# A planned transformer block: loads in a fixed order on two queues, pads on ScalarE, first projections by piece

## The chip, the cores and the metric

The kernel runs on one core of a Trainium2 chip. A core has TensorE (matrix products into PSUM, called PE in the profile), VectorE (DVE), ScalarE (ACT), GpSimd (POOL) and SyncE (SP), which run side by side and wait for each other through semaphores, and 16 DMA engines, which are given work through the queues of SP and ACT. The metric is the time of one launch in microseconds (us), the median of several runs.

## The reference

The block works on x of 2048 rows by 448 columns in bfloat16, with 16 heads of 28. Cut to what is computed:

```python
mod = (silu(c) @ w_mod).reshape(1, 6, 1, -1)          # c: 1 x 448, w_mod: 448 x 2688
sa, ca, ga, sb, cb, gb = (mod[:, i] for i in range(6))
h = layernorm(x) * (1 + ca) + sa
x = x + ga * A(h)          # attention, output projection wo
h = layernorm(x) * (1 + cb) + sb
x = x + gb * B(h)          # (sigmoid(h @ w_gate) * (h @ w_up)) @ w_down, 1792 wide

# A, for each of 4 segments s of 512 rows, per head (phi(t) = t + 1 for t > 0, else exp(t)):
a_dot = softmax(qs @ ks.T * scale + causal_mask) @ vs
a_mem = (phi(qs) @ M) / (phi(qs) @ z + 1e-6)
o = sigmoid(beta) * a_mem + (1 - sigmoid(beta)) * a_dot
M = M + phi(ks).T @ vs;  z = z + phi(ks).sum(rows)
```

## The kernel before

The kernel is a list of nodes for a planner (class `Graph`, L61 to L202). Each node is one piece of work for one engine (or for the better of two), with a duration in ns, the nodes it depends on, the buffers it takes (`Slot`) and a priority. `Graph.run` plays the engines forward with these durations and writes the instructions out in the order in which its nodes started. Every engine then runs its own instructions strictly in that order. So the order on each engine, the queue of SP included, is set when the kernel is built, from the table `PRM` (a priority for each kind of work and segment) and from estimates such as a load's bytes by a rate. `lock` keeps a VectorE node and a GpSimd node from being planned at the same time.

The work of a segment is:

- `ln1`: statistics (L543, L544), inverse root on GpSimd (L550, L551), normalized rows `xn` (L556). Segment 0 is turned by TensorE (L612) and scaled and shifted out of PSUM (L622, L624). Segments 1 to 3 are turned by DMA transposes on SP (L566), scaled and shifted in place (`modulated`, L576, L578), and copied by two more DMAs so that each half of the partitions holds other columns ("shifts", L583, L586).
- `proj`: Q and K (L654), 64 rows of the array for each half, and V (L667).
- `attention`: for four chunks of four heads, logits (L732), exponentials on ScalarE (L746, L752), causal masks on GpSimd (L759) or VectorE (L762); then `unit`: the product with V (L787, "PV"), the memory part (L798) and eight VectorE steps up to the transposed output `oT` (L836). There are 16 units.
- `memory`: phi of the keys, a DMA transpose on SP (`pk`, L690), a product (L696), and copies or sums into `M_sb`; TensorE and VectorE have these in their order too.
- `wo_ln2`: output projection (L850), residual (L853), second norm, turned by DMA like `ln1`.
- `ffn`: gate and up (L869), tanh (L874), product (L876), down projection (L888), residual (L894), store.

Loads are issued where the planner puts them: a load waits until the planned backlog of the DMA is under 1.5 us, so that loads and transposes alternate on SP. Weights of Q, K and V are loaded into halves of 64 partitions, gate into the lower half and up into the upper. Weights of the output and down projections are scaled by ga and gb once (L528, GpSimd or VectorE). GpSimd also fills pads (L402 to L406), and makes masks. wq and wk are spread into `wqk` by copies (L494, L496). Fourteen matmuls on zeros come first (L901).

Of the kernel before, what the change touches and what calls it, by code (L numbers as in the profile page):

```python
# [13 lines left out]
P = 128  # L14
ENGINES = ("PE", "ACT", "DVE", "POOL", "SP")
SWITCH = 100
LAND = 1400
BACKLOG = 1500

PRM = {  # L20
    "lg": (342668, 163718, 862290, 444708),
    "ex": (11292, 58782, -81945, -99549),
    "mask": (714759, 688992, 570356, 838873),
    "wo": (-115857, 165597, 132082, 82856),
    "ln2": (34672, 175804, -62256, 229718),
    "tanh": (49047, 57056, -189565, -190444),
    "f": (459427, 351186, 97650, 519018),
    "dn": (-246990, 125472, 5139, -149550),
    "phi": (347979, 71782, 70153, 194215),
    "t": (177082, 2744, 97268, 333494),  # L30
    "ln1": (103674, -21841, -146667, -66581),
    "mem": (-329139, -251836, -266191, -362099),
    "pj": (46451, -491526, -367702, 12439),
    "ot": (260037, 371245, 206466, 283138),
    "ev": (-163934, -86827, -16960, -49902),
    "gu": (231026, 437056, 117153, 563291),
}
STAY = 3248
# [22 lines left out]
class Graph:  # L61


    LAG = {"PE": {"PE": 0, "ACT": 205, "DVE": 205, "POOL": 205, "SP": 205},
           "ACT": {"PE": 200, "ACT": 0, "DVE": 170, "POOL": 190, "SP": 170},
           "DVE": {"PE": 180, "ACT": 150, "DVE": 0, "POOL": 170, "SP": 120},
           "POOL": {"PE": 150, "ACT": 110, "DVE": 90, "POOL": 0, "SP": 100}}
# [22 lines left out]
    def ready_at(self, n, e):  # L90
        t = n.release
        if n.move is not None and n.move > 300:
            t = max(t, self.ring - BACKLOG)
        for d in n.deps:
            t = max(t, d.end + d.lag + self.gap(d.eng, e))
        return t

# [30 lines left out]
    def run(self):  # L128
# [10 lines left out]
        self.ring = 0.0  # L139
        order, t, done = [], 0.0, 0  # L140
        while done < len(self.nodes):
            moved = False
            for e in ENGINES:
# [6 lines left out]
                narrow = None  # L150
                for n in ready:
                    got = self.place(n, t, narrow)
# [5 lines left out]
                    for s, i in zip(n.take, got):  # L158
                        s.at = i
                        for w in range(s.width):  # L160
                            self.free[s.pool][i + w] = float("inf")
# [10 lines left out]
                    if n.move is not None:  # L172
                        self.ring = max(self.ring, n.end) + n.move
                        n.lag = self.ring - n.end + LAND
# [4 lines left out]
                    for s in {id(x): x for x in (*n.take, *n.use)}.values():  # L179
                        if all(u.end is not None for u in s.users):  # L180
                            f = max(u.end + (u.lag if u.move is not None else 0) for u in s.users) + 120
                            for w in range(s.width):
                                self.free[s.pool][s.at + w] = f
# [9 lines left out]
            times = [x for x in (*at.values(), held) if x > t]  # L193
            times += [r for e in ENGINES for n in avail[e] if (r := self.ready_at(n, e)) > t]
            times += [f for fs in self.free.values() for f in fs if t < f < float("inf")]
# [10 lines left out]
def kernel(  # L206
# [36 lines left out]
    NWARM = 14  # L243
# [34 lines left out]
    c_col = const.tile([CP, NK], BF16, name="c_col")  # L278
# [4 lines left out]
    beta_t = const.tile([P, NHC, 4], BF16, name="beta_t")  # L283
# [4 lines left out]
    cols = const.tile([P, 4, 2, NK], F32, name="cols")  # L288
# [12 lines left out]
    xn_r = ring("xn", NXN, [P, HR + NK * P], BF16)  # L301
# [23 lines left out]
    silu_bc = U_r[0:CP, 0].rearrange("p i b e j -> p (i b e j)")[:, 0:NK * P].rearrange("p (k o) -> p k o", o=P)  # L325
    fT_flat = fT_r[:].rearrange("p n l -> p (n l)")
# [3 lines left out]
    def load(eng, dst, src, size, deps=(), prio=0, use=(), take=(), rate=230.0):  # L330
        def fn():
            (nc.sync if eng == "SP" else nc.scalar).dma_start(dst, src)
        return add(eng, 520, fn, deps, prio=prio, use=use, take=take, move=size / rate)

    def pr(kind, s):
        return PRM[kind][s]
# [13 lines left out]
    def load_x(eng, t0, t1, prio):  # L350
        n = load(eng, x_sb[:, t0:t1, :], x_dram[t0 * P:t1 * P, :].rearrange("(t p) d -> p t d", p=P),
                 (t1 - t0) * P * D * 2, prio=prio)
# [5 lines left out]
    def load_wm(eng, j0, nj, flat, prio, deps=()):  # L358
        t = flat[0:CP, 0:NK * nj * D].rearrange("p (k n) -> p k n", k=NK)
        n = load(eng, t, wm_cols[:, :, j0 * D:(j0 + nj) * D], CP * NK * nj * D * 2, prio=prio, deps=deps,  # L360
                 rate=230.0 if nj == 1 else 300.0)
# [4 lines left out]
    def load_half(eng, dst, half, w, prio, c0=0, c1=NC, rate=200.0):  # L366
        r = slice(half * HR, (half + 1) * HR)
        n = w.shape[1]
        return load(eng, dst[r, c0:c1, 0:n], w[c0 * HR:c1 * HR, :].rearrange("(c p) n -> p c n", p=HR),
                    HR * (c1 - c0) * n * 2, prio=prio, rate=rate)  # L370

    l_c = load("SP", c_col[:], c.rearrange("o (p k) -> p (o k)", p=CP), 20000, prio=2 * BIG)
    load_x("SP", 0, 1, 2 * BIG - 100)
    load_x("ACT", 1, 2, 2 * BIG - 100)
    load_x("SP", 2, 3, 2 * BIG - 200)
    load_x("ACT", 3, 4, 2 * BIG - 200)
    load_wm("SP", 0, 2, pT_r[:].rearrange("p n h w -> p (n h w)"), 2 * BIG - 300)
    W_qk = [load_half("ACT", wqk_st, 0, A_wq, 2 * BIG - 300), load_half("SP", wqk_st, 1, A_wk, 2 * BIG - 400)]
    W_v = [load_half("SP", wvv, i, A_wv, BIG - 60) for i in range(2)]
    lp = BIG - 100  # L380
    load_x("SP", TPS, 2 * TPS, lp)
    l_beta = load("SP", beta_t[:], A_beta.partition_broadcast(P), 8000, prio=lp - 1)
# [8 lines left out]
    def pads_fn():  # L391
        nc.vector.memset(xn_r[:, :, 0:HR], 0.0)
        nc.vector.memset(xn_r[:, :, HR + D:], 0.0)
        nc.vector.memset(wqk[:, :, :, Dh:HP], 0.0)

    wz = qT_r[:, 0, 0, :]
    n_wz = dve(200, lambda: nc.vector.memset(wz, 0.0), prio=BIG)
    n_ident = pool_op(700, ident_fn, prio=BIG)
    n_pads = dve(300, pads_fn, prio=BIG - 1, lock=True)

    def vpad_fn(i):
        nc.gpsimd.memset(vt_r[:, i, :, :, Dh:HP], 0.0)  # L402
        nc.gpsimd.memset(vt_r[:, i, :, :, Dh:Dh + 1], 1.0)
    n_vpad = [pool_op(700, lambda i=i: vpad_fn(i), prio=BIG - 5) for i in range(NV)]
    n_wopad = pool_op(1500, lambda: nc.gpsimd.memset(wo_sb[:], 0.0), prio=BIG - 4)
    n_opad = pool_op(400, lambda: nc.gpsimd.memset(O_r[:, :, :, Dh:HP, :], 0.0), prio=BIG - 6)  # L406
    l_wo = [load("SP", wo_sb[h * HP:h * HP + Dh, :, :],
                 A_wo.rearrange("(c h e) n -> h e c n", h=4, e=Dh)[h], Dh * NHC * D * 2, [n_wopad], prio=lp - 4)
            for h in range(4)]
# [11 lines left out]
    n_masks = pool_op(1900, masks_fn, prio=BIG - 7)  # L421
# [11 lines left out]
    n_hsel = pool_op(900, hsel_fn, prio=BIG - 9)  # L433


    def silu_fn():
        nc.vector.tensor_scalar(th[:], th[:], 0.5, 0.5, op0=ALU.mult, op1=ALU.add)
        nc.vector.tensor_tensor(silu[:], th[:], c_col[:], ALU.mult)
    n_th = act(200, lambda: nc.scalar.activation(th[:], c_col[:], AF.Tanh, scale=0.5), [l_c], prio=BIG)
    n_silu = dve(220, silu_fn, [n_th], prio=BIG, lock=True)  # L440
    n_sbc = dve(340, lambda: nc.vector.tensor_copy(
        silu_bc, silu[:].rearrange("p (k o) -> p k o", o=1).to_broadcast([CP, NK, P])), [n_silu], lock=True)

    def mod_cols(j, vi, both, prio):
        b = bank()

        def mm():
            for kc in range(NK):
                r = P if kc < NK - 1 else HR
                for k in range(NK):  # L450
                    nc.tensor.matmul(pf(b)[0:r, kc:kc + 1], lhsT=wm_at[j][:, k, kc * P:kc * P + r],
                                     rhs=silu[:, k:k + 1], start=(k == 0), stop=(k == NK - 1))
            for kc in range(NK if both else 0):
                for k in range(NK):
                    if kc:
                        nc.tensor.matmul(pf(b)[:, NK + kc:NK + kc + 1], lhsT=wm_at[j][:, k, kc * P - HR:kc * P + HR],
                                         rhs=silu[:, k:k + 1], start=(k == 0), stop=(k == NK - 1))
                    else:
                        nc.tensor.matmul(pf(b)[HR:P, NK:NK + 1], lhsT=wm_at[j][:, k, 0:HR], rhs=silu[:, k:k + 1],
                                         start=(k == 0), stop=(k == NK - 1), tile_position=(0, HR))  # L460
        n = add("PE", (32 if both else 16) * 40, mm, [n_silu, wml[j]], take=[b], prio=prio, mode="F")

        def ev():
            parts = [(0, NK - 1, P, 0), (NK - 1, NK, HR, 0)] + ([(NK, NK + 1, P, 1), (NK + 1, 2 * NK, P, 1)] if both else [])
# [479 lines left out]
```

## Time and profile before

| What | Value |
|---|---|
| Median of 3 runs | 270.43 us (269.98 to 270.99) |
| Profiled execution, its own time | 269.01 us |
| Its span, first to last instruction | 267.3 us |
| TensorE busy | 236.7 us (89%) |
| VectorE busy | 201.2 us (75%) |
| ScalarE busy | 153.6 us (57%) |
| GpSimd busy | 56.4 us (21%) |
| Read from HBM | 11.07 MB |

The page of a profile gives busy time of each engine, then the same in 40 slices, the DMA queues, the chain of work that ended last, and the costliest groups of instructions with the mean duration of one and the idle time before them. A busy TensorE may still run slowly, since the profile counts a matmul as busy from its start to its modelled end, and since its clock (PEclk) can be at half. Durations in the page come from this one execution.

### The profile page before, as it was taken

How to read it: one execution, taken by the hardware profiler on the slowest of the kernel's cores; microseconds unless marked ns; L12 is line 12 of the kernel's file. 1: busy time of each engine (PE TensorE's matmuls, PEld its weight loads, DVE VectorE, ACT ScalarE, POOL GpSimd, SP SyncE). 2: the span in 40 equal slices, each digit the busy share in tenths (PEclk: the TensorE clock that was granted, in tenths of full speed). 3: DMA queues.
4: the chain of work that ended last, by engine and by line, in shares of the span. 5: the costliest groups of instructions: out<-in, count | busy, mean ns of one | idle time of the engine just before them, and what ended most of it. 6: DMA issues, size and time to landing. Idle time of an engine off the chain costs nothing. (4 is left out here: it accounts for less than half of the span.)

```text
span 267.3 us, 5480 instructions
## 1 busy us (share of the span) xinstructions
PE 236.7 (89%) x2130; PEld 108.0 (40%) x2130; DVE 201.2 (75%) x478; ACT 153.6 (57%) x182; POOL 56.4 (21%) x110
## 2 busy tenths in 40 slices
PE   7289936999862899989999999999999999899995
PEld 2253512443330334435644443564444435354342
DVE  5658895998999798999699998769967674243331
ACT  1266964999986668974689834577534223033210
POOL 6701340111673570006020003400000211000000
PEclk9958965999995599999999999999999999999999
DMA  4999999999021333400432113130010212400011
GB/s 115 186 228 221 141 189 210 205 203 331 14 42 39 70 60 67 64 16 6 80 88 56 22 20 76 40 89 20 17 37 0 22 39 54 105 0 2 1 33 35
DMA packets 34737, 21.71 MB, mean 81 GB/s; under 512 B 23000, under 2 KB 32920, under 8 KB 34712
## 3 DMA queue, kind: packets, MB, share of 16 engines
q1 hardware_dynamic: 33960, 20.74, 38.5%
q10 hardware_dynamic: 752, 0.63, 0.9%
q8 instruction: 16, 0.26, 0.4%
q14 instruction: 9, 0.07, 0.1%
HBM read 11.07 MB, written 1.84 MB: 48 GB/s over the span
## 5 line engine op out<-in xcount | busy, mean ns | idle before, releaser
L869 PE MATMUL ps<-hT,wgu 64*128 64x512 bf16 x784 | 93.4, 383 | 1.1 <-DMA hT<-hT 0.8
L874 ACT ACTIVATE tt<-ps 128x512 f32<-128x512 f32 x56 | 33.3, 595 | 61.2 <-PE ps L869 60.5
L746 ACT ACTIVATE pT<-ps 128x2048 bf16<-128x2048 f32 x32 | 60.0, 1878 | 9.6 <-PE ps L732 8.7
L869 PEld LDWEIGHTS <-wgu 64*128 64x128 bf16 x784 | 40.4, 95 | 49.1 <-issue 12.8
L876 DVE SCALAR_TENSOR_TENSOR fT<-tt,ps 128x512 bf16<-128x512 f32 x56 | 38.1, 683 | 27.6 <-ACT tt L874 26.7
L888 PE MATMUL ps<-wd_sb,fT 128*128 128x448 bf16 x224 | 45.8, 353 | 0.2 <-ACT aT L804 0.2
L654 PE MATMUL ps<-hT,wqk 64*128 64x512 bf16 x224 | 31.0, 413 | 3.3 <-DMA hT<-hT 1.6
L759 POOL TENSOR_SCALAR_AFFINE_SELECT pT<-pT 128x512 bf16<-128x512 bf16 x25 | 15.9, 647 | 83.3 <-ACT pT L746 63.8
L888 PEld LDWEIGHTS <-fT 128*128 128x128 bf16 x224 | 20.7, 98 | 21.8 <-issue 4.4
L550 POOL TENSOR_SCALAR rs<-mv 128x1 f32<-128x1 f32 (+1 forms) x23 | 5.4, 237 | 78.8 <-DVE mv L544 78.7
L732 PE MATMUL ps<-qT,kT 28*128 28x512 bf16 (+3 forms) x256 | 17.0, 320 | 4.8 <-ACT pT L752 2.6
L543 DVE BATCH_NORM_STATS2 st<-x_sb 128x6 f32<-128x448 bf16 x32 | 19.5, 609 | 2.0 <-DMA x_sb<-in_A_x_dram 1.7
L654 PEld LDWEIGHTS <-wqk 64*128 64x128 bf16 x224 | 13.5, 100 | 18.3 <-issue 9.9
L894 DVE TENSOR_TENSOR ot<-ps,x_sb 128x448 bf16<-128x448 f32 x16 | 9.8, 615 | 10.9 <-PE ps L888 10.6
L762 DVE TENSOR_TENSOR pT<-pT,cmask 128x512 bf16<-128x512 bf16 x39 | 16.6, 450 | 1.2 <-ACT pT L746 0.9
L556 DVE TENSOR_SCALAR xn<-x_sb,mv,rs 128x448 bf16<-128x448 bf16 x32 | 14.7, 490 | 2.8 <-POOL rs L551 2.8
L850 PE MATMUL ps<-wo_sb,oT 128*128 128x448 bf16 x64 | 14.3, 354 | 1.4 <-DVE fT L876 0.8
L752 ACT ACTIVATE pT<-ps 128x2048 bf16<-128x2048 f32 x8 | 15.0, 1879 | 0.7 <-PE ps L732 0.6
L551 POOL TENSOR_TENSOR rs<-rs,mhalf 128x1 f32<-128x1 f32 (+1 forms) x23 | 14.9, 646 | 1.9
L787 PE MATMUL ps<-pT,vt 128*32 128x512 bf16 (+3 forms) x256 | 12.3, 315 | 3.0 <-DVE pT L762 3.0
L732 PEld LDWEIGHTS <-kT 28*128 28x128 bf16 x256 | 5.0, 94 | 22.4 <-issue 22.0
L667 PE MATMUL ps<-wvv,hT 64*128 64x448 bf16 x112 | 12.0, 350 | 0.2 <-ACT pT L746 0.2
(96 smaller groups left out, 249.3 us busy)
## 6 DMA issues: line engine op xcount, KB each, us to landing
hT<-hT SPq DMA_DIRECT2D x7, 256.0 KB, 3.4
out_dram<-ot SPq DMA_DIRECT2D x16, 112.0 KB, 1.7
x_sb<-in_A_x_dram SPq DMA_DIRECT2D x3, 448.0 KB, 11.4
wgu<-in_B_w_gate_dram SPq DMA_DIRECT2D x3, 448.0 KB, 5.2
wgu<-in_B_w_up_dram SPq DMA_DIRECT2D x3, 448.0 KB, 6.4
hT<-hT SPq DMA_DIRECT2D x7, 192.0 KB, 2.7
wd_sb<-in_B_w_down_dram SPq DMA_DIRECT2D x2, 448.0 KB
pT<-in_w_mod_dram SPq DMA_DIRECT2D x1, 784.0 KB
```

What stands on the lines that cost most here:

```text
L543: nc.vector.bn_stats(st_r[:, st.at, :], src)
L551: nc.gpsimd.tensor_tensor(r, r, mhalf[:, 0:w], ALU.pow)
L654: nc.tensor.matmul(pf(b), lhsT=w, rhs=chunk(hT, cc, half), start=(cc == 0), stop=(cc == NC - 1))
L732: nc.tensor.matmul(ps[:, lg.at + hs, o:o + nq], lhsT=kT_r[r, k.at, hcs[u], kb * P:(kb + 1) * P], rhs=qT_r[r, q.at, hcs[u], kb * P:L], star ...
L746: nc.scalar.activation(pT_r[:, pTs[units[0]].at, :, w0:w0 + L], ps_, AF.Exp, scale=scale)
L752: nc.scalar.activation(dst, ps_.rearrange("p h (u w) -> p u h w", u=2), AF.Exp, scale=scale)
L759: nc.gpsimd.affine_select(out=blk, in_=blk, compare_op=ALU.is_ge, fill=0.0, base=0, pattern=[[0, 4], [1, P]], channel_multiplier=-1)
L762: nc.vector.tensor_tensor(blk, blk, cmask[:].rearrange("p (o k) -> p o k", o=1).to_broadcast([P, 4, P]), ALU.mult)
L869: nc.tensor.matmul(pf(b), lhsT=wgu[half * HR:(half + 1) * HR, cc, fs], rhs=chunk(hT, cc, half), start=(cc == 0), stop=(cc == NC - 1))
L874: a = act(485, lambda gp=gp, tt=tt: nc.scalar.activation(tt_r[:, tt.at, :], pf(gp), AF.Tanh, scale=0.5), [n], use=[gp, tt], prio=pr("tanh" ...
L876: f = dve(597, lambda up=up, tt=tt, ft=ft: nc.vector.scalar_tensor_tensor(fT_r[:, ft.at, :], tt_r[:, tt.at, :], 1.0, pf(up), op0=ALU.add, ...
L888: nc.tensor.matmul(pf(b)[:, 0:D], lhsT=fT_r[:, fts[fc].at, t * P:(t + 1) * P], rhs=wd_sb[:, fc, :], start=(fc == 0), stop=(fc == NFC - 1))
```

## The change

All loads are written in one fixed order of priority (`first(i)`), on two queues, and a load's landing time is now a number written by hand (`land`) in place of bytes by a rate. The order is c, x of segment 0, the first two parts of w_mod (half on each queue), wq and wk, x of segment 1 and wv (both on two queues), the third part of w_mod, x of segment 2, wo, beta, two more parts of w_mod, gate (ACT) and up (SP), the last part of w_mod, x of segment 3, w_down. The planner no longer holds loads back for the backlog. c and beta come as one row each and are turned into columns, or spread over partitions, by small matmuls. Pads are filled by ScalarE (`fill`), the memset of `wo_sb` and those of `xn` go to VectorE. Segment 1 is turned by TensorE as segment 0 is (`PE_LN1`), `hT` is used in seven pieces of 128 rows (`piece`, `chunk_of`), and the first projections of a segment are split (`job`): in segment 0 into seven pieces for three of the four head chunks. Modulations, head masks of the memory (`rm`) and the `wqk` copies may be placed on GpSimd too (`shared`, `vec`). Priorities are now given to each instance of a kind of work, a node that two engines can do may wait for the quicker one, and durations and lags are new. Thirty-two smaller matmuls on zeros take the place of fourteen, most with low priority.

```diff
-SWITCH = 100
-LAND = 1400
+SWITCH = 96
+LAND = 1600
...
 PRM = {
-    "lg": (342668, 163718, 862290, 444708),
...
+    "lg": (779407, 690680, 1007126, 586007, 525675, 887224, 290547, 103150, 41521, 384483, 1940342, 1914149, 1902869,
...
         t = n.release
-        if n.move is not None and n.move > 300:
-            t = max(t, self.ring - BACKLOG)
+        if n.move is not None and n.move > 100000:
+            t = max(t, self.ring[e] - BACKLOG)
...
+                    if len(n.durs) > 1 and any(max(at[o], t) - t + d * COST[o] < n.durs[e] * COST[e]
+                                               for o, d in n.durs.items() if o != e):
+                        continue
...
-    NWARM = 14
+    NWARM = 16
+    NP = 7
+    PE_LN1, PE_LN2 = (1,), ()
...
-        return add(eng, 520, fn, deps, prio=prio, use=use, take=take, move=size / rate)
+        n = add(eng, 600, fn, deps, prio=prio, use=use, take=take)
+        return add("SP", 0, None, [n], prio=prio, release=land * 1000)
...
-    l_c = load("SP", c_col[:], c.rearrange("o (p k) -> p (o k)", p=CP), 20000, prio=2 * BIG)
...
+    l_c = load("SP", c_row, c, 3.2, prio=first(0))
+    for t, e in enumerate(("SP", "ACT", "SP", "ACT")):
+        load_x(e, t, t + 1, first(1 + t), 3.8 + 0.25 * t)
+    load_wm(0, 2, pT_r[:].rearrange("p n h w -> p (n h w)"), first(5), (6.1, 7.6))
+    W_qk = [load_half("ACT", wqk_st, 0, A_wq, first(6), 9.8), load_half("SP", wqk_st, 1, A_wk, first(6), 10.2)]
+    load_x("SP", TPS, TPS + 2, first(7), 11.4)
+    load_x("ACT", TPS + 2, 2 * TPS, first(7), 11.4)
+    W_v = [load_half(e, wvv, i, A_wv, first(8), 14.4) for i, e in enumerate(("SP", "ACT"))]
...
-    n_vpad = [pool_op(700, lambda i=i: vpad_fn(i), prio=BIG - 5) for i in range(NV)]
-    n_wopad = pool_op(1500, lambda: nc.gpsimd.memset(wo_sb[:], 0.0), prio=BIG - 4)
-    n_opad = pool_op(400, lambda: nc.gpsimd.memset(O_r[:, :, :, Dh:HP, :], 0.0), prio=BIG - 6)
...
+        return act(dur, lambda: nc.scalar.activation(dst, src, AF.Identity, bias=value), [n_wz], prio=prio)
+    n_pads = fill(wqk[:, :, :, Dh:HP].rearrange("p c h e -> p (c h) e"), 0.0, 560, 2 * BIG)
+    n_wopad = dve(560, lambda: nc.vector.memset(wo_sb[:], 0.0), prio=BIG - 1e6, lock=True)
+    n_vpad = [fill(vt_r[:, i, :, :, Dh + 1:HP].rearrange("p t h e -> p (t h) e"), 0.0, 380, BIG) for i in range(NV)]
...
+    def c_cols():
+        for k in range(NK):
+            nc.tensor.matmul(pf(b_c)[0:CP, k:k + 1], lhsT=steps(c_row[:, k:k + CP], [NK, CP]), rhs=ones[:, 0:1],
+                             start=True, stop=True)
...
+    load_wm(2, 1, fT_flat[:, 2 * NK * D:], first(10), (17,))
+    load_x("SP", 2 * TPS, 3 * TPS, first(11), 19)
+    l_wo = [load("SP", wo_sb[h * HP:h * HP + Dh, :, :], A_wo.rearrange("(c h e) n -> h e c n", h=4, e=Dh)[h], 22,
+                 [n_wopad], prio=first(12)) for h in range(4)]
+    l_beta = load("SP", beta_row[:], A_beta.rearrange("(o h) -> o h", o=1), 23, prio=first(13))
+    load_wm(3, 2, fT_flat, first(14), (25,))
+    W_gu = []
+    for i, (c0, c1) in enumerate(((0, 4), (4, NC))):
+        W_gu.append(load_half("SP", wgu, 1, B_w_up, first(15 + i), 34 + 4 * i, c0, c1))
+        W_gu.append(load_half("ACT", wgu, 0, B_w_gate, first(15 + i), 34 + 4 * i, c0, c1, [xl[2 * TPS]]))
+    load_wm(5, 1, fT_flat[:, 3 * NK * D:], first(17), (39,))
+    load_x("SP", 3 * TPS, 4 * TPS, first(18), 41)
...
+            hs.append(add(("DVE", "ACT", "POOL"), (322, 720, 850), mod, [*trs] + ([n_sb, n_cb] if vi else [n_sa, n_ca]), use=[hT],
+                          prio=prio(), lock=True))
...
+    def piece(hT, i, half):
+        return hT_r[half * HR:(half + 1) * HR, hT.at, i, :]
...
+    def job(prio, hn, deps, fn, first, use, split, per):
+        n = None
+        for i, (p0, p1) in enumerate(split):
+            n = add("PE", per * (p1 - p0), lambda p0=p0, p1=p1: [fn(p) for p in range(p0, p1)],
+                    [*(d for p in range(p1) for d in hn[p]), *deps, n], take=first if i == 0 else (),
+                    use=use if i == 0 else [*first, *use], mode="H", prio=prio())
+        return n
...
+        if s in PE_LN1:
+            return turned([layer_norms([x], [l], lambda: pr("ln1", s))[0] for x, l in tiles], hT, 0,
+                          lambda: pr("ln1", s), False)
...
+        split = tuple((i, i + 1) for i in range(NP)) if s == 0 else ((0, 3), (3, NP))
...
+            rm_n[(s + 1, hc)] = shared((200, 430), lambda e, hc=hc, rm=rm: vec(e).tensor_tensor(
+                rm_r[:, rm.at, :], M_sb[:, hc, :], bmask[:], ALU.mult), [u, n_masks], take=[rm], prio=pr("mem", s))
```

## The prediction

> **What bounds the kernel now.** I read the page's 40 slices first, then the busy time by stage, then the waits inside the two bad stages.
>
> ```profile
> PE   7289936999862899989999999999999999899995
> DVE  5658895998999798999699998769967674243331
> PEclk9958965999995599999999999999999999999999
> ```
>
> Each digit is a slice of 6.68 us. TensorE is full from slice 14 on; its holes and its half-speed clock all lie in the first 95 us. VectorE is at 8 or 9 nearly everywhere until slice 30.
>
> ```profile
> 0.00:18.00 18.00, 10.24 (x111) 6.03 (x112) 10.39 (x32) 5.43 (x8) 9.31 (x33) 0.83 0.86 172
> 24.00:48.00 24.00, 16.95 (x192) 7.34 (x188) 18.59 (x50) 17.65 (x20) 6.88 (x9) 0.79 1.13 190
> 66.00:96.00 30.00, 20.52 (x188) 8.17 (x187) 27.54 (x63) 21.69 (x22) 17.88 (x26) 0.77 0.20 44
> 108.00:204.00 96.00, 94.13 (x861) 45.07 (x857) 83.19 (x200) 63.21 (x76) 12.88 (x26) 1.00 0.20 42
> 57.30:108.00 50.70, 41.09 (x414) 17.04 (x410) 45.87 (x107) 39.98 (x41) 22.93 (x32) 0.87 0.40 96
> 116.50:205.50 89.00, 87.59 (x796) 42.23 (x796) 76.37 (x183) 55.38 (x66) 12.88 (x26) 1.00 0.19 43
> ```
>
> (Stretch, its length, then busy PE, PEld, DVE, ACT, POOL, clock, DMA share, GB/s.) In 66 to 96 VectorE is busy 27.5 of 30 us while TensorE is not: VectorE is late. From 108 to 204 it is the other way: TensorE 94.1 of 96, VectorE 83.2.
>
> A busy TensorE is not a dense one, so I price its work from unbroken pieces of the chain of waits:
>
> ```profile
> 172.89 1.32 PE ps L667 x14
> 177.23 1.20 PE ps L787 x32
> 182.50 3.13 PE ps L869 x28
> 256.12 7.88 PE ps L888 x41
> ```
>
> That is 94 ns a matmul for V, 37 for PV, 112 for gate, up, Q and K, 190 for down and output projection. With the counts of the groups (L869 784, L654 224, L888 224, L850 64, L667 112, L787 256) and some 16 us of small ones, the dense work is 207.2 us. The last matmul ends at 264.0, so 57 us are lost, and 3.3 us follow it.
>
> ```profile
> 40.93 0.58 PE L654 MATMUL ps<-hT,wqk 64*128 64x512 bf16 x1 [1.31 <-ACT pT L746]
> 43.05 3.14 PE L654 MATMUL ps<-hT,wqk 64*128 64x512 bf16 x13 [1.55 <-DMA hT<-hT]
> 106.98 0.73 PE L787 MATMUL ps<-pT,vt 128*32 128x512 bf16 x16
> ```
>
> The third line is the eighth attention unit's PV (the last of segment 1). In the order of the instructions 53.3 us of dense work lie before its end, which comes at 107.6: 54 us lost. The 153.9 us behind it take 156.4. So everything to be won lies before this PV; call its end T8.
>
> **Where transfers wait.** Times to landing on the SP queue (KB, median us):
>
> ```profile
> x_sb<-in_A_x_dram SPq DMA_DIRECT2D x3, 448.0 KB, 11.4
> fT<-in_w_mod_dram SPq DMA_DIRECT2D x1, 784.0 KB, 11.6
> hT<-xn SPq DMA_TRANSPOSE x28, 2.5
> ```
>
> Loads are issued 11 us and more ahead of landing. Anything issued behind them on SP comes behind their bytes: the transpose of 46.8 us took 6.6 to land, against 2.5 when the queue is empty. "hT<-hT" (256 KB) takes 3.4.
>
> ```profile
> 18.00:20.00 2.00, 1.94 (x9) 0.71 (x9) 1.14 (x3) 1.95 (x4) 0.00 (x0) 0.50 1.15 213
> 62.00:64.00 2.00, 2.00 (x19) 0.71 (x13) 1.80 (x7) 2.00 (x3) 0.00 (x0) 1.00 1.08 362
> ```
>
> The DMA engines are full in both, at 213 GB/s (weights into 64 partitions) and at 362 (w_down and x, 128 partitions).
>
> **What the Trainium skill says.** "SBUF — State Buffer", section "SBUF: two separate sides": a transfer into partitions 0 to 63 reaches half the ports (196 GB/s measured there, 328 for all 128), and two transfers at once, one per half, gave only 6% more. The trace agrees on the first (213 and 362) and has no pair of halves. The same section: VectorE and GpSimd share one pair of ports, and the loser blocks for the whole instruction. The trace agrees: "th" (L437), on 4 columns, took 1.84 us at 10.47 beside a 1.59 us GpSimd memset. "DMA: Bandwidth & Descriptors", section "Queues, rings and completion order": on each engine a queue's descriptors are taken in order. The landings above agree.
>
> **The change part by part.**
>
> Start. The first w_mod piece (784 KB) lands at 13.9 now, behind it wk at 15.4, and the first projection starts at 17.26. After, x and half of w_mod lie on each queue: 0.23 + 0.40 MB, just what the ACT queue carries now with wq, which landed at 9.5. c (112 pieces of 8 B) and beta (128 of 32 B) become single rows; DMA moved only 77 GB/s from 4 to 6 us, so this may give 1 us. wq and wk follow: 0.8 MB at 206 GB/s, 3.9 us, so 13.4. First projection: 14 to 15, a gain of about 3. ScalarE's nine pad fills: by L494 (784 columns, 0.84 us) and L510 (16, 0.21), between 2 and 4 us; it idles 5.75 us there now, but six DMA issues (0.45 to 0.7 each, 2.2 if the queue is full as SP's at 4.22) come first. If they push "th" past 9.5 us the start loses up to 2. The wo_sb memset leaves GpSimd, so "th" costs 0.2. Projections by piece and 32 warm-up matmuls in place of 14: the 28 matmuls of 17.3 to 23.3, mostly at half clock, took 6.0 us against 3.1. Up to 2.9, below nothing only if the fills are late.
>
> Segment 1 turned by TensorE: plus 32 transposes of 57 ns (1.8 us dense), plus 3 VectorE reads of PSUM (0.54) less 4 of "hT<-hT" (0.44), minus 4 DMA transposes and two shifts: the 1.55 us wait at 43.05 and the half clock behind it have no cause left.
>
> Loads. All 11.07 MB are now issued before any transpose on SP. At the rates of the trace: x of segment 0 to 3.8 us; w_mod 0.80 MB at 209, 3.8; wq, wk 3.9; x 0.46 at 272, 1.7; wv 3.8; w_mod 1.9; x 1.7; wo 1.9; w_mod 0.80 at 230, 3.5; gate and up 3.21 at 213, 15.1; w_mod 1.9; x at 350, 1.3; w_down 1.61 at 350, 4.6. End: 49 us. Then come, at 1.2 us each (26.27: four in 5.2 us): two pk, four transposes of segment 2, the third pk, landing at 57 to 58. TensorE's order has the third memory product (at 29.2 us of its work) and segment 2's Q and K behind these, and VectorE the copy of M_sb. It waits there: by rows times mean duration in its new order it has done 43.0 us of work, so the whole gain at the start is idled away.
>
> From there to T8 the new order asks VectorE for 37.6 us more (to 80.6, the last mask of unit 8). At the 94% that it reaches when late (16.9 of 18 us in 72 to 90) that is 40 us: T8 = 58 + 40 + 0.5 = 98.5, against 107.6. TensorE has 56.2 us of work before it, ScalarE 71; neither limits. Before, VectorE had 45.9 us to do in this stretch (57.3 to 108): the gain is that work put later.
>
> Behind T8. TensorE has 152.8 us left, VectorE 91.1 to the last transposed O (oT). Means overrate this stretch: for before they give 80.2 between the same marks where the trace has 77.2. So 87.7, at 94% 93.3 us: 191.8. Output projection of segment 3, 16 matmuls: 195.3. Behind it TensorE has 59.5 us; with 1.1 for a late hT and more switches, 255.9; tail 3.3: span 259.2. VectorE's total is unchanged (202 against 201 by the same means), so modulations, rm and scalings on GpSimd (56 us busy, now about 60) give nothing by themselves. Two gate loads on ScalarE's queue sit behind the first exponential and wait for segment 2's x; behind them stands the second exponential. That x lands at 20.6 by the sum above and the first exponential ends near 21.5 (23.91 + 1.88 now, less some 4), so the wait is nothing and the issues cost 1.3 us; each us that x is later would cost TensorE's next logits one.
>
> **Sum.** 259.2 against 267.3. The profiled execution took 269.01, 1.7 more than its span; the median is 270.43. In proportion: 262.3.
>
> **Rivals.**
>
> B, the halves do overlap: wq/wk, wv and gate/up (4.8 MB) at 300 instead of 210 GB/s take 16 in place of 22.8 us, the loads end at 42, T8 is 92: 255.5. For: each queue writes its own 64 partitions. Against: the skill's 6%, and 205 GB/s from 6 to 8 us with both queues busy.
>
> C, same: VectorE and TensorE are now nearly equal behind T8 (87.7 and 84.1 us until unit 16), where TensorE had 93.8 to VectorE's 77.2. If VectorE reaches only the 87% of 108 to 204, this adds 7.5: 269.8.
>
> D, slower: the SP queue. Transposes wait for all loads; every us by which these end later moves T8. Break-even is T8 at 106.8, loads ending at 57 (195 GB/s throughout; the trace has 188 over the first 57 us, transposes included). At 60 it is 273.5. For: the trace's mean. Against: transposes of 256 B pieces slowed that mean, and none is left in the loads.
>
> That the order doesn't come out as said is excluded: the instruction lists show the loads first.
>
> **How the numbers follow.** A (the forecast, own range 257 to 267) 0.47, B 0.25, C 0.13, D 0.15. A measurement here tells 0.5% from no change, so same is 269.1 to 271.8. Faster: A, B and a third of C, 0.76; same 0.10; slower 0.14. Range: from B with less port contention (252) into the beginning of D (271.5).
>
> **What would show it.** First projection matmul at 14 to 15; last w_down byte at 49 (42 for B, 57 or more for D); the third memory product near 58; unit 8's PV ending at 98.5; VectorE over 93% busy from there to the last oT near 192. If VectorE is idle behind T8 with TensorE full, or TensorE waits with the loads long landed, the working is wrong.

## The result and the profile after

The changed kernel takes 294.08 us (median of 4 runs, 292.1 to 294.98) against 270.21 for the kernel before on the same chip. The ratio is 1.088, with a 95% interval of 1.081 to 1.094: it is slower by 24 us where 262.3 was forecast. The span of the profiled execution is 290.4 us (before 267.3, forecast 259.2).

The kernels below were timed in several sessions, always beside the kernel before (medians 269.68 to 270.21 there). Medians are over all runs, ratios over those within 1.5% of a kernel's fastest, so that for a kernel whose runs spread the two can point differently. Differences of about 1 us between sessions mean nothing.

The slices of the page of the changed kernel, now 7.26 us each:

```profile
PE   8800089987598696998899999998999999999995
DVE  5490006999989998899974999996989944414331
PEclk9955579999689977799999999999999999999999
GB/s 198 218 225 223 216 227 141 83 38 91 84 72 3 82 73 64 18 2 18 78 116 2 18 52 33 2 33 47 59 34 0 3 87 81 16 18 16 19 16 47
```

Each of TensorE and VectorE has three slices of zeros: TensorE from 15 to 36 us, VectorE from 22 to 44. From 24 to 36 us no engine computes anything, while the loads go on at 219 GB/s. This is no engine at its limit. By stretches (length, then busy PE, PEld, DVE, ACT, POOL, clock, DMA share, GB/s):

```profile
18.00:24.00 6.00, 0.00 (x0) 0.00 (x0) 3.36 (x10) 0.00 (x0) 3.09 (x8) 0.50 1.11 224
24.00:36.00 12.00, 0.00 (x0) 0.00 (x0) 0.00 (x0) 0.00 (x0) 0.00 (x0) 0.50 1.06 219
36.00:42.00 6.00, 4.39 (x22) 1.66 (x24) 0.00 (x0) 0.00 (x0) 0.00 (x0) 0.62 0.93 291
```

What ends it stands in TensorE's timeline of the same execution (start, length, instruction, and in brackets the idle time before it and who ended it):

```profile
11.44 3.06 PE L745 MATMUL ps<-ident,xn 128*128 128x128 bf16 x32
37.61 3.14 PE L1058 MATMUL ps<-x_sb 128*128 128x448 bf16 x8 [23.10 <-DMA x_sb<-in_A_x_dram]
40.68 3.63 PE L805 MATMUL ps<-hT,wqk 64*128 64x512 bf16 x32
```

L1058 are the warm-up matmuls. Their result is never read; they are there only to keep the clock up. But their zero operand (L494) is now the last tile of `x_sb`, where x of segment 3 is loaded. The planner puts 24 of the 32 matmuls ahead of segment 0's transposes and 8 behind them, and these 8 come after that load in the order of the program. So they read what the load writes and must wait for it: it was issued on SP at 24.47, the nineteenth load of that queue, and landed at 37.6. The first projection is behind them in TensorE's order, and though its operands had been ready since about 18 us it stood there until 40.68, behind 8 matmuls whose result nobody needs.

### The profile page after: what moved, and what is told of

Its sections match the earlier page's. It is cut to its first block, busy times and chain, and to the rows that moved or that the text cites. A ratio compares the mean times of both kernels' runs of the same rounds, so it can differ in the third digit from the quotient of the medians.

```text
span 290.4 us, 5584 instructions
## 1 busy us (share of the span) xinstructions
PE 245.0 (84%) x2185; PEld 108.0 (37%) x2185; DVE 203.7 (70%) x472; ACT 152.8 (53%) x186; POOL 62.4 (21%) x119
## 5 line engine op out<-in xcount | busy, mean ns | idle before, releaser
L1023 PE MATMUL ps<-hT,wgu 64*128 64x512 bf16 x784 | 96.3, 383 | 3.8 <-DVE fT L1030 1.5
L1042 PE MATMUL ps<-wd_sb,fT 128*128 128x448 bf16 x224 | 46.8, 353 | 0.0
L1058 PE MATMUL ps<-x_sb 128*128 128x448 bf16 x32 | 10.3, 495 | 24.3 <-DMA x_sb<-in_A_x_dram 23.1
L805 PE MATMUL ps<-hT,wqk 64*128 64x512 bf16 x224 | 28.9, 395 | 1.0 <-ACT pT L897 1.0
L788 ACT CAST kT<-ps 128x512 bf16<-128x512 f32 x11 | 6.5, 587 | 29.6 <-PE ps L805 29.4
L790 DVE CAST kT<-ps 128x512 bf16<-128x512 f32 x5 | 3.4, 675 | 24.6 <-PE ps L805 24.6
L805 PEld LDWEIGHTS <-wqk 64*128 64x128 bf16 x224 | 11.6, 98 | 15.8 <-issue 6.2
L560 POOL TENSOR_TENSOR rs<-rs,mhalf 128x1 f32<-128x1 f32 (+1 forms) x26 | 15.9, 613 | 2.2
L817 PE MATMUL ps<-wvv,hT 64*128 64x448 bf16 x112 | 13.3, 365 | 1.7 <-DVE vt L790 1.5
L559 POOL TENSOR_SCALAR rs<-mv 128x1 f32<-128x1 f32 (+1 forms) x26 | 6.2, 238 | 39.7 <-DVE mv L553 36.9
```

Of the source, the lines that this page charges most:

```text
L560: nc.gpsimd.tensor_tensor(r, r, mhalf[:, 0:w], ALU.pow)
L805: nc.tensor.matmul(pf(b), lhsT=w, rhs=piece(hT, i, half), start=(i == 0), stop=(i == NP - 1))
L1023: nc.tensor.matmul(pf(b), lhsT=wgu[half * HR:(half + 1) * HR, chunk_of(i, half), fs], rhs=piece(hT, i, half), start=(i == 0), stop=(i == N ...
L1042: nc.tensor.matmul(pf(b)[:, 0:D], lhsT=fT_r[:, fts[fc].at, t * P:(t + 1) * P], rhs=wd_sb[:, fc, :], start=(fc == 0), stop=(fc == NFC - 1))
```

## The experiments

**Is it the operand?** Three kernels, timed together. In the first the zeros lie in a slice of qT that is not written before segment 2:

```diff
-    wz = x_sb[:, NSEG * TPS - 1, :]
+    wz = qT_r[:, NQ - 1, NHC - 1, 0:D]
```

> The zero operand of the warm-up matmuls moves from x_sb to a slice of qT that is written only in segment 2; every engine's order stays. Theory W (the last 8 warm-up matmuls wait for the load of segment 3's x into the same tile, and everything waits behind them on TensorE): those 8 run between 14.5 and 18 us, the first projection matmul starts at 18 to 19 instead of 40.68, nothing else changes, so about 22 us go: span 267 to 270, time 270 to 273. Rival Q (the loads would hold the work up anyway until 42 us, since transposes and segment x stand behind them on SP): the first projection is early as well, but TensorE and VectorE wait again before 50 us and less than 12 us go: time 282 or more. Rival F (apart from this wait the forecast holds): time 262.

Measured: 272.64 us, ratio to before 1.010 (1.007 to 1.013), span 270.2. TensorE's timeline of this run:

```profile
9.64 2.05 PE L604 MATMUL ps<-silu,pT 112*128 112x1 bf16 x62 [1.19 <-DMA pT<-in_w_mod_dram]
11.55 4.16 PE L745 MATMUL ps<-ident,xn 128*128 128x128 bf16 x32
15.50 2.70 PE L1058 MATMUL ps<-qT 128*128 128x448 bf16 x8
18.14 3.63 PE L805 MATMUL ps<-hT,wqk 64*128 64x512 bf16 x32
```

The wait is gone, the first projection comes at 18.14 instead of 40.68, and 21.4 us of the time go with it. Theory W holds; neither rival does. (In the second line the 32 transposes take 4.16 us, with a granted clock of 0.50 from 12 to 16 us.)

In the second the operand stays and the 8 late matmuls go:

```diff
-        for _ in range(2):
+        for _ in range(2 if i < 12 else 0):
```

> The zero operand stays in x_sb; the last 8 of the 32 warm-up matmuls are not issued, their places in the plan stay. Theory W: no instruction of TensorE in front of the first projection reads x of segment 3 any more, so the first projection starts at 17.5 to 18.5 and the time is that of the first run within 1.5 us, a little more if the clock is lower in the first projections without them. Rival (the stall comes from something else, such as the projection's own operands or the SP queue): first projection still after 37 us, time about 294.

Measured: 273.82 us, 1.014 (1.006 to 1.022). The first projection starts at 16.86, without 8 matmuls before it, but its 32 matmuls take 6.20 us at a granted clock of 0.61 instead of 3.63 at 1.00: they end 1.3 us later than in the first run. The times of the two runs do not tell them apart; by the traces the late warm-ups do what they are for, and only what they read was wrong.

In the third the operand is segment 2's last tile, whose load lands earlier:

```diff
-    wz = x_sb[:, NSEG * TPS - 1, :]
+    wz = x_sb[:, 3 * TPS - 1, :]
```

> The zero operand becomes the last tile of segment 2 in x_sb instead of segment 3; every engine's order stays. That load is issued at 9.62 us and landed 13.5 later, at 23.1. Theory W: the 8 warm-up matmuls start when it lands, at 23 to 23.5, the first projection follows 3.1 us later at about 26.3, 14.4 us earlier than with segment 3: time about 280, some 8 above the first run. Rival (another cause): first projection and time as in the changed kernel, 40.7 and 294.

Measured: 283.44 us, 1.048 (1.040 to 1.057). The direction was right and the size was not: the first projection came at 35.7, not at 26.3. The waits of this run before 40 us show why:

```profile
PE ps L1058 <- DMA x_sb<-in_A_x_dram: 16.9, 1, 16.9
DVE th L578 <- ACT th L587: 15.9, 1, 15.9
ACT vt L511 <- DMA x_sb<-in_A_x_dram: 15.6, 1, 15.6
```

The load of segment 2 is placed earlier in the program, so more stands behind it: most of the warm-ups and some of ScalarE's pad fills, which copy from the same zeros. The wait ended at 22.6, as expected, but the modulation columns, the transposes and the fills were all still to do then. What counts is when the load lands and also what is queued behind it.

**Why 272.6 and not 262.3?** All the following runs start from the first one. First the loads: w_down moves on SP from before the first pk transposes to behind the two hT shifts of segment 2 (its nodes are taken out of the order and put back there; every other engine's order is as it was).

> On the kernel with its own zeros; the four loads of w_down (1.6 MB) are issued on SP after the two hT shifts of segment 2 instead of before the first pk transposes; order on all other engines unchanged. In the first run SP was done with the w_down loads at 41.8, the transposes behind them landed from 49 on and the third memory product came at 54.0. Theory S (what the start gains is idled away behind the loads on SP, as the prediction had it): transposes issued from about 39, third memory product at 45 to 47, TensorE's loss between 48 and 60 falls from 9 us to about 4, unit 8's PV at 96 to 98 instead of 101.8, time 4 to 6 below the first run, 267 to 269. Rival V (VectorE sets the pace there in any case: it was idle for only some 3.5 of the 12 us from 42 to 54): 0 to 3 us, time 270 to 272.5.

Measured: 271.85 us, 1.006 (1.002 to 1.011). The third memory product comes at 52.65 instead of 54.01, unit 8's PV starts at 100.95 instead of 101.06. SP's longest wait and two stretches of this run:

```profile
SPq L848 <- DVE pq L840: 16.4, 1, 16.4
```

```profile
42.00:48.00 6.00, 6.00 (x76) 2.55 (x72) 5.83 (x19) 5.86 (x9) 0.00 (x0) 1.00 0.78 141
48.00:54.00 6.00, 2.22 (x32) 1.36 (x25) 5.69 (x19) 4.53 (x5) 1.90 (x3) 0.97 0.34 70
```

With the loads out of its way SP stood 16.4 us waiting for VectorE's pq, and VectorE was busy 11.5 of the 12 us. In the first run it was busy 8.4 of them and stood 3.2 us for memory products whose transposes were behind the w_down loads on SP. That wait is gone here, but the edit brings another. The two waits (us in total, times, longest), of the first run and of this one:

```profile
DVE M_sb L854 <- PE ps L847: 3.2, 2, 2.7
```

```profile
DVE wd_sb L686 <- DMA wd_sb<-in_B_w_down_dram: 3.6, 1, 3.6
```

VectorE's order has a scaling of w_down after 61.1, and its load was now issued only from 55.6 on; VectorE stood there until 64.8. So the 1.3 us gained at the third product are gone by unit 8, and this run does not decide between S and V: the wait that S names is real, and what would be won without the later load is not shown. In the first run and the six others with the loads in their old place and an early start, the third product came at 54.0 to 56.2, and VectorE stood 2.1 to 5.4 us for it.

Then GpSimd. Fifteen scalings of wo and w_down by the gates are left out on GpSimd:

```diff
-            vec(e).tensor_tensor(w[:, k, :], w[:, k, :], rep[:, i, :], ALU.mult)
+            if e == "DVE":
+                vec(e).tensor_tensor(w[:, k, :], w[:, k, :], rep[:, i, :], ALU.mult)
```

> On the kernel with its own zeros; the 15 scalings of w_down and wo that run on GpSimd (15.6 us) are left out, those on VectorE stay; so most rows of the two weights are not multiplied by the gates. Order unchanged. Theory G (GpSimd's port use stretches VectorE's instructions: phi's L831 took 387 and 412 ns behind T8 where before it took 280 and 286, O<-U 466 against 386): VectorE's busy time falls from 202.9 to 198 to 200, the time by 1.5 to 3 to about 270. Rival N (GpSimd's work is free, as the prediction had it): VectorE's total within 1 us of 202.9, time within 1 us of the first run.

Measured: 269.22 us, 0.996 (0.992 to 1.000), 3.4 us below the first run by the medians and 1.6 by the spans of the profiled executions. VectorE, from whose list nothing was taken, is busy 196.9 us instead of 202.9. A row of VectorE (line, output<-inputs, count, busy us and mean ns), for the kernel before:

```profile
L680 DVE TENSOR_SCALAR e<-qT 128x512 bf16<-128x512 bf16 x12 | 3.8, 313 | 0.0
```

for the first run:

```profile
L831 DVE TENSOR_SCALAR e<-qT 128x512 bf16<-128x512 bf16 x12 | 5.2, 435 | 0.0
```

and for the run without the scalings:

```profile
L832 DVE TENSOR_SCALAR e<-qT 128x512 bf16<-128x512 bf16 x12 | 3.6, 302 | 0.0
```

The same instruction on the same operands takes 302 ns in the mean or 435, depending on what GpSimd does. The median is 286 ns in both runs; the means differ by a few instructions that run beside a scaling, and of which the longest took 1.12 us. Two such in the first run (the other, pq, usually takes 0.43 us):

```profile
93.50 2.06 POOL L681 TENSOR_TENSOR wd_sb<-wd_sb,rep 128x448 bf16<-128x448 bf16 x2
93.65 1.02 DVE L831 TENSOR_SCALAR e<-qT 128x512 bf16<-128x512 bf16 x1
94.78 1.06 DVE L833 TENSOR_TENSOR pq<-e 128x512 bf16<-128x512 bf16 x1
```

Theory G holds: 6.0 us of stretch for 15.6 us of GpSimd's work, 0.38 for each. In the profiled execution the time was won behind T8 (last oT 201.0 instead of 202.5), not ahead of it: T8 is 101.9 where it was 101.8, though VectorE had 3.6 us less to do up to there. Two runs use the price. The modulations and rm that the change gave to GpSimd go to VectorE (`vec(e)` becomes `nc.vector` in L702 and L860):

> On the kernel with its own zeros; the 5 modulations and 6 products rm that the change gave to GpSimd (7.3 us there) are done by VectorE at the same places; the scalings stay on GpSimd. By the run without scalings, 15.6 us of GpSimd's work stretched VectorE by 6.0 us, 0.38 us for each. Theory G (the stretch pays back what is moved): VectorE gains 5 x 0.41 + 6 x 0.29 = 3.8 us of work and loses 0.38 x 7.3 = 2.8 us of stretch, so its busy time is 203 to 204.5 and the time within 1.2 us of the first run, 271.4 to 273.8. Rival N (GpSimd's work costs VectorE nothing; what is moved there is won): VectorE 206.7, time 2 to 3 higher, 274.6 to 275.8.

Measured: 274.14 us, 1.017 (1.008 to 1.026); VectorE 205.0 us. The busy time rose by 2.1, where 3.8 us of work without any relief would have given 3.8: the relief is some 1.7 us for 7.3 us of GpSimd's work, less than the price of the scalings. But in six executions of kernels with one and the same list VectorE was busy between 201.8 and 203.7 us, and the interval of the time takes in the first run's; the time lies between the two bands. So what the move is worth, and G or N for it, stay open.

The same for the scalings (L681):

> On the kernel with its own zeros; the 15 scalings of wo and w_down on GpSimd (15.6 us) are done by VectorE at the same places instead (0.384 us each, 5.8 us). Theory G: 5.8 us more work, 6.0 us less stretch: VectorE's busy time within 1 us of 202.9, time within 1.5 us of the first run, 271.1 to 274.1. Rival N: VectorE 208.7, and at the 0.56 to 0.76 us of time for each us of VectorE that the run with repeated gating instructions showed, 276 to 277.

Measured: 270.86 us, 0.998 (0.995 to 1.002); VectorE 201.7 us with 15 more instructions than in the first run. The busy time is 1.2 us below the first run's where N has 208.7, so 5.8 us of work cost nothing: G again. (The ratio rests on 11 of 20 runs; the median lies above the 269.68 of the kernel before in that session.)

Last, who sets the pace behind T8? VectorE gets 28 more instructions (the gating of segments 0 and 1 repeated on 128 columns), or TensorE gets 56 more matmuls (the first two of each gate and up group done twice):

```diff
+                for w in (L, P) if s in (0, 1) else (L,):
+                    nc.vector.scalar_tensor_tensor(fT_r[:, ft.at, 0:w], tt_r[:, tt.at, 0:w], 1.0, pf(up)[:, 0:w],
+                                                   op0=ALU.add, op1=ALU.mult)
```

> On the kernel with its own zeros; each gating instruction L1030 of segments 0 and 1 is followed by a repetition on 128 of its 512 columns, 28 more VectorE instructions of about 0.2 us, 6 us in all, nearly all between 88 us and the last oT. Theory V (VectorE sets the last oT, as the prediction had it, though only 88% busy): the last oT and the time move by 5 to 6 us, time 277 to 279. Rival P (the plan's waits and TensorE set the pace behind T8, and VectorE has 12 us of slack there): at most 2 us, time 272.5 to 274.5.

```diff
-                for half, b in ((0, gp), (1, up)):
+                for m, (half, b) in enumerate(((0, gp), (1, up)) * (2 if i == 0 and s in (0, 1) else 1)):
```

> On the kernel with its own zeros; the first two matmuls of each gate and up group of segments 0 and 1 are done twice, 56 more matmuls of 112 ns, 6.3 us in all, between 88 us and the last oT. Theory V (VectorE sets the last oT; TensorE loses 10 us between 102 and 204): at most 3 us more, time 273 to 275.5. Rival P (TensorE sets the pace, what it loses there belongs to its own order): 5 to 6.5 more, time 277.5 to 279.

Measured: 277.09 us (1.028, 1.022 to 1.033) and 277.24 us (1.030, 1.024 to 1.035). The repeated gating was dearer than expected:

```profile
L1032 DVE SCALAR_TENSOR_TENSOR fT<-tt,ps 128x128 bf16<-128x128 f32 x28 | 8.0, 287 | 1.0
```

So 8.0 us on VectorE moved the last oT by 6.2 us (202.5 to 208.7) and the time by 4.5; 6.3 us on TensorE moved the last oT by 4.2 and the time by 4.6. A part of this was there before: T8 came at 102.7 and 103.5 in these executions, against 101.8, so from T8 to the last oT they took 5.2 and 2.6 us longer. Neither V nor P alone: by the times both engines are charged for more than half of what they are given, though VectorE is idle for 12 of the 100.7 us there.

**Is there a better version?** The kernel before, with its 14 scalings on GpSimd done by VectorE at the same places:

> The kernel before, with its 14 scalings of wo and w_down on GpSimd (14.5 us there) done by VectorE at the same places instead. Theory G (the port's stretch is a property of the pair of engines and not of the new plan): VectorE's busy time stays within 1.5 us of the 201.2 before, GpSimd falls to 42, the time is 0 to 2 us lower, 268 to 270. Rival N: VectorE has 14 x 0.38 = 5.3 us more to do, the time rises by 2 to 4, 272 to 274.

Measured: 268.67 us, 0.995 (0.993 to 0.998). VectorE 200.6 us (before 201.2), GpSimd 42.1 (before 56.4). Of the versions that do all the work it is the only one whose median and ratio are both below the kernel before, by 0.46%, with the interval clear of 1. It also shows that the kernel before had the stretch: with 5.3 us more on its list VectorE is busy 0.6 us less, so the 14.5 us of scalings had cost it 5.9. And the changed kernel with three of the edits:

> The changed kernel with its own zeros, w_down loaded late and the scalings on VectorE, the three edits together. If the three gains add (21.4, 0.8 and 1.8 us): 270.0, no difference from the kernel before that can be told. If the two small ones are the same microseconds of VectorE, 271 to 272.5.

Measured: 270.95 us (median of 14 runs, 266.2 to 308.6). The ratio of 0.994 (0.990 to 0.997) rests on 6 of them, and the median is above the 269.89 of the kernel before in that session, so no more is claimed than that it is level with the kernel before, as expected.

## Why the prediction was wrong

**The step that failed** is the last of "Start": "Projections by piece and 32 warm-up matmuls in place of 14 [...] Up to 2.9, below nothing only if the fills are late." It counted the warm-ups as time on TensorE and did not ask what they read. The first run prices the wait at 20.2 us of span (290.4 to 270.2). None of the rivals had it; D was slower too, but by transposes behind loads on SP, which is not what made this kernel slow. The span was missed by 31.2 us; the other 11.0 lie between 270.2 and 259.2, and are followed on the first run: 3.3 up to T8, 7.4 from there to the last oT, 0.3 behind it.

**The first projection at 14 to 15** came at 18.14 in the first run. w_mod landed at 9.6, but the 32 transposes took 4.16 us at half clock, and VectorE waited 2.5 us for wk. The fills on ScalarE did no harm: what TensorE waited for was w_mod (1.19 us, in the timeline above), 4.3 us earlier than before. In seven executions whose order is the same up to there the first projection came anywhere from 14.60 to 18.14; in the run with more matmuls, where the clock was 1.00, the same transposes took 2.63 us. So the forecast was met in part of the executions and not in others.

An early start was lost again, though, and by a cost that the prediction named and put at nothing. In the run with w_down late the first projection came at 15.67 and the first exponential ended at 22.9; then ScalarE's queue has:

```profile
24.07 2.51 ACTq L429 DMA_DIRECT2D wgu<-in_B_w_gate_dram  x2
26.62 1.88 ACT L904 ACTIVATE pT<-ps 128x2048 bf16<-128x2048 f32 x1 [3.77 <-DMA wo_sb<-in_A_wo_dram]
```

The two gate loads may be issued only when x of segment 2 has landed (23.4 here; 21.3 to 23.4 in the seven executions, where 20.6 was forecast), and the second exponential stands behind them: 3.8 us where the forecast had 1.3. (The bracket puts the end of the wait down to wo's load; by the program it is x of segment 2 that the gate loads depend on, and in all seven they were issued 0.3 to 0.7 us after its landing.) TensorE waited 2.48 us for that exponential here, 0.85 to 2.38 in four others, and not at all in the two that had started at 18. Segment 1's transposes began at 28.1 to 31.2 in all of them, whenever the first projection had come.

**Loads ending at 49.** The last byte of w_down landed at 48.1 in the first run. The sum was right by luck, since its terms were wrong both ways: x of segment 2 landed at 22.5 instead of 20.6 and w_mod behind it at 28.3 instead of 26.0; then gate and up took 9.7 us (up landed at 38.0) instead of 15.1, part of gate having gone beside w_mod; and the rest took 10.1 instead of 7.8. A stretch of the changed kernel in which up alone was loaded, and one of the first run with gate beside it (the last number is GB/s):

```profile
27.00:35.00 8.00, 0.00 (x0) 0.00 (x0) 0.00 (x0) 0.00 (x0) 0.00 (x0) 0.50 1.05 201
```

```profile
30.00:36.00 6.00, 5.33 (x90) 3.20 (x88) 5.44 (x18) 5.00 (x9) 2.57 (x4) 1.00 1.03 306
```

Gate writes partitions 0 to 63 from ScalarE's queue, up 64 to 127 from SP's: 306 GB/s together against 201. The prediction took from the Trainium skill ("SBUF — State Buffer", section "SBUF: two separate sides") that two such transfers gain 6%; here they gain 52%, and the measurement decides for these loads. The other pairs of halves gained nothing: from 10 to 18 us of the first run, with wq, wk and wv on the two queues (and a part of x), the rate was 219 GB/s. What makes the difference was not tried, nor whether the gain comes from the two halves or from the two queues. In the changed kernel itself this did not come about, since the gate loads stood behind the stalled exponential on ScalarE and were issued at 44.7. Rival B's overlap is thus shown for these two loads; the end of the loads at 42 that it needed is not.

**"the whole gain at the start is idled away"** and the third memory product "near 58" as the mark that T8 hangs on. The product came at 54.0, and VectorE stood 3.2 us there behind the loads: the mechanism was there, and smaller than forecast. At the mark that the prediction counted to, the last mask of unit 8, VectorE was at 98.61 with 82.0 us done, where 98.0 and 80.6 were forecast. That this came so near is luck: the product was 4.0 us early, and from there VectorE needed 44.6 us instead of 40. T8 was 101.8 (PV 101.06 and 0.73) against 98.5: 0.6 of the 3.3 us come from the mask, and 2.7 from TensorE, which has two memory products and fourteen gate and up matmuls in its order ahead of that PV, where the forecast put 0.5 us in all:

```profile
98.47 1.04 PE L949 MATMUL ps<-pq,rm 128*128 128x512 bf16 x2
99.44 1.69 PE L1023 MATMUL ps<-hT,wgu 64*128 64x512 bf16 x14
101.06 0.73 PE L938 MATMUL ps<-pT,vt 128*32 128x512 bf16 x16
```

The mark was also misread in the kernel before. In TensorE's order there the PV at 106.98 is the ninth of sixteen; the eighth is this one:

```profile
99.26 0.73 PE L787 MATMUL ps<-pT,vt 128*32 128x512 bf16 x16
```

It ends at 100.0, so a T8 of 98.5 was to be 1.5 us earlier than before and not 9, and the measured 101.8 is later. (The dense work is misadded as well: its prices and counts give about 204 us, not 207.2.) The forecast of the end was summed from the work behind the mark, and does not hang on this.

**Segment 1 turned by TensorE** did what was said: there is no wait for a shifted hT before segment 1's Q and K, and TensorE lost 6.7 us of dense work between 24 and 48 where it had lost 12.3 (the 24 us less the dense work in them, by the counts and prices of the prediction). It is part of the gain that was lost again in the waits after it.

**"modulations, rm and scalings on GpSimd [...] give nothing by themselves"**, and "VectorE's total is unchanged". The total came as forecast (202.9 against 202), but GpSimd's work is not free in it: 6.0 us are the stretch by the scalings. The skill's statement in the same section, that the loser of the ports that VectorE and GpSimd share blocks for the whole instruction, agrees with the lines shown (1.02 us where 0.29 is usual); the page limits it to VectorE instructions that use the shared pair. The prediction cited it for the start and then used means of the kernel before, which hold 5.9 us of the same stretch, all of it ahead of 98.6 us, where the scalings of that kernel lie.

**VectorE at 94% behind T8**, 93.3 us to the last oT. In the first run:

```profile
101.20:203.00 101.80, 98.46 (x917) 44.68 (x910) 89.74 (x201) 69.15 (x79) 24.23 (x41) 1.00 0.17 35
```

VectorE is busy 89.7 of 101.8 us, 88%, with TensorE busy 98.5. From T8 to the last oT, 101.8 to 202.5, it is busy 88.7 of 100.7 us, 7.4 longer than forecast. The work is 1.0 more than the 87.7 of the forecast, 94.4 us at 94%; the other 6.3 are waiting. (Six of the 15 scalings, 6.4 us of GpSimd, lie here; without them VectorE's work is 86.4.) This is rival C, nearly at its price of 7.5. The runs with added work agree with it: the two engines have nearly equal work and wait for each other by turns, and both are charged. The rest is right: from the last oT to the end 67.7 us against 67.4.

Of the two marks for being wrong, VectorE idle behind T8 with TensorE full came true in the first run. The other did not fire as it was written: in the changed kernel TensorE waited for a load that was still under way, and whose bytes it did not need.

## What to carry to other kernels

An instruction whose result nobody reads still waits for what it reads: before a scratch operand is put into a tile that a load fills, look where its last reader stands in the order against that load, and what is queued behind that reader. When the bound engine's work is moved to GpSimd, charge it for the stretch before the gain is counted (for the scalings 0.38 us for each us of GpSimd here, 0.41 in the kernel before; for modulations and rm less, and not resolved). Where two engines have nearly the same work left, do not forecast with the better one's best share: what was added to either of them here was paid for more than half. And where a mark is set on an engine's instruction, count what other work lies ahead of it in that engine's order.

## What was not expected of the hardware

Loads into the two halves of the partitions on two queues ran at 306 GB/s together, against 201 while one half was written alone; wq, wk and wv, written in the same way, showed no such gain. A VectorE instruction with a mean of 302 ns (128x512 bf16) had a mean of 435 ns beside a busier GpSimd, with the median at 286 in both: a few of the instructions took over 1 us. And the gating instruction on a quarter of its columns took 287 ns against 681 on all of them; an estimate from these two sizes alone is that some 156 ns of it (287 less a third of the difference) do not depend on the columns.
